# One core, attention with a mixture of experts and a gated MLP behind it: the last head pair in two parts, combine work in late attention, eight output staging buffers, one pass for two w_in quarters, a new order

## The chip, the cores and the metric

The kernel runs on one core of a Trainium2 chip. The metric is the time of one execution on the device in microseconds (us). Five engines work side by side, each through its own list of instructions in order: TensorE (PE; its weight loads are shown apart as PEld), VectorE (DVE), ScalarE (ACT), GpSimd (POOL) and SyncE (SP), which here issues the DMAs. An instruction that waits for another engine holds up everything behind it on its own.

## The reference

Three layers follow each other. Each line is computed in fp32 on 2304 tokens (4 batches of 576) of width 512.

```
scores = q @ k.T / sqrt(64)              # 4 batches x 8 heads, 576 x 576, head size 64
mask:  heads 0-3: 0 <= i-j < 32          # a local window
       heads 4-7: 0 <= i-j < 128 and (i-j) % 4 == 0     # the same, dilated by 4
attn = softmax(masked scores) @ v        # -> x, 2304 x 512
logits = x @ phi                         # 32 slots, 8 experts x 4
slot_in = softmax(logits, over the 2304 tokens).T @ x
slot_out[e] = relu(slot_in[e] @ w1[e]) @ w2[e]          # w1 512 x 1024, w2 1024 x 512
x = softmax(logits, over the 32 slots) @ slot_out
h = x @ w_in;  out = (h * sigmoid(h)) @ w_out           # 512 x 2048, 2048 x 512
```

## The kernel before

**Attention.** A local and a dilated head of a batch make a head pair; there are 16, n = 4b + p. With the dilated head's positions sorted by their rest, both become windows of 64 keys over nine blocks of 64 rows. For each pair: SP loads k, q and v (`lk`, `lq`, `lv`); POOL spreads q into two half-filled tiles (`qx`, `qy`); `vx` (POOL) and `vy` (DVE or ACT) write v twice; PE adds masks and scores (`M`, `S`); DVE takes the row maximum (`rm`); ACT the nine exponentials with their sums (`ex`); DVE the reciprocal (`rc`, L238 and L239), POOL the product with it (`nm`, L242), DVE four transposes (`pt.0` to `pt.3`, L249 to L255); PE multiplies by v (`pv.0`, and `pv.1` for block 0); ACT evicts (`xe`, L280 and L282); PE transposes (`T`, L293) and takes the logits (`lt`); ACT evicts the tokens (`te`).

**Dispatch and combine.** Per batch, `da`, `dt`, `dm`, `db`, `dq`, `dr`, `dsub`, `dex`, `dc`, `dw`, `dacc` and `ds` carry a running softmax over tokens; the last `ds3` gives the slot inputs (`sit`, `sie`). `caa` to `cag` compute the softmax over slots, split into a high and a low part (`cad`, L383; `caf`, L388 and L389). `cb{b}.0` and `cb{b}.1` transpose it on PE for three and for two token tiles (L404), and `cbs` evicts that to `ct`.

**Experts.** `L1.0` to `L1.15` and `L2.0` to `L2.15` run all slots through the experts' halves, with the weights streaming in; `ht` transposes between them, `sotm` behind.

**MLP.** The combine is not done on its own: w_in is multiplied by the slot outputs (`aq`, one eighth of the hidden columns for each q) and stacked as a high and a low part (`ah`, `al`, `ac`, tile `astk`), so that `h` is one matmul of 384 tokens. The weights arrive as 64-bit words and are turned into fp32 by three DVE operations each (`cva`, `cvb`, `cvi` for w_in; `cvc`, `cvd`, `cvo` for w_out: L594, L596, L598); w_out is split too (`wh` on ACT, `wl` on DVE). The work goes in six groups G, of six token tiles and eight hidden tiles f each (groups 0 to 2 with f 0 to 7, groups 3 to 5 with f 8 to 15). A unit is one f for 384 tokens: `h` on PE, `si` on ACT (L758, silu), `gh` on ACT or DVE and `gl` on DVE (L763, L765, L768: the gated value and what its rounding leaves), then three `om` matmuls per token tile (the first unit's are `on`) into six banks. At a group's end `oe` evicts: groups 0 to 2 to `part`, groups 3 to 5 added to it (L850) into an output tile `ost`, from which `do` (SP) stores. There are four places in `ost`.

**What sets the order.** Each piece is an `op` with a name, an engine, a planned cost and the names it depends on. `list_schedule` (L985) plays them through with the costs and the latencies `LAT`, takes on every engine the one with the longest remaining path plus the bonus of its kind in `PRIO`, and keeps PSUM banks apart; `ATT` gives the order of SP's loads. The program then has each engine's instructions in that order. Neither costs nor bonuses are in the program itself.

All matmuls but the transposes and those of `cb` (L404) go through one helper, `mm` (L83), so its line stands for most of PE.

## Time and profile before

| what | us |
|---|---|
| three runs | 367.99, 369.27, 369.54 (median 369.27) |
| the profiled execution | 368.79 |
| its span | 367.0 |
| PE busy in it | 347.6 (95%) |
| DVE busy | 234.6 (64%) |
| ACT busy | 165.9 (45%) |
| POOL busy | 75.3 (21%) |
| granted clock of PE, mean | 0.999 |

The span is the program from its first to its last instruction on the chip; busy times of different engines overlap. In time the program is attention to about 95 us, dispatch to 101, experts to 134.6, the first group of the MLP from 138 to 178 and the other five groups to 363; the last store ends the span at 367.0. A matmul of the 2.4 GHz clock is shown with its modelled end, so the duration of one overlaps with the next; the distance from start to start is the pace.

### The profile page before, as it was taken

The numbers are of one execution on the slowest core, as the hardware profiler recorded it, in microseconds if no ns is written. First come the engines' busy times: TensorE is split into PE (matmuls) and PEld (weight loads), VectorE is DVE, ScalarE is ACT, GpSimd is POOL, SyncE is SP. The second block draws the span as 40 slices with busy tenths as digits, with TensorE's granted clock in tenths as the row PEclk, the third lists the DMA queues.
The fourth block names the chain that finished last, engine by engine and source line by source line (L and its number), as shares of the span: only waits on it lengthen the run. The fifth ranks groups of instructions, "written<-read, shape, count | busy, mean of one in ns | idle before, by whom it ended". The sixth has DMA issues, their size and how long they took to land.

```text
span 367.0 us, 8152 instructions
## 1 busy us (share of the span) xinstructions
PE 347.6 (95%) x3209; PEld 267.6 (73%) x3212; DVE 234.6 (64%) x540; ACT 165.9 (45%) x558; POOL 75.3 (21%) x120
## 2 busy tenths in 40 slices
...
GB/s 258 411 405 404 408 403 402 405 397 287 374 361 424 412 417 417 330 133 0 280 121 59 0 2 0 1 2 0 3 0 0 116 57 0 2 116 56 2 0 171
DMA packets 17461, 70.03 MB, mean 191 GB/s; under 512 B 1936, under 2 KB 2448, under 8 KB 11664
## 3 DMA queue, kind: packets, MB, share of 16 engines
...
q8 instruction: 25, 0.41, 0.5%
q14 instruction: 12, 0.10, 0.1%
HBM read 64.80 MB, written 4.72 MB: 189 GB/s over the span
## 4 chain that ended last, share of the span: by engine, by line
PE 88%; DVE 4%; ACT 3%; issue 2%; POOL 1%; DVEq 0%; ACTq 0%
PE ps L83 85%; PE ps L293 3%; ACT rt_px L226 1%; ACT rt_px L280 1%; PE ps L404 1%; DVE stats L221 1%; DVE w_ost L850 1%; POOL rv_v L189 1%; ACT rt_px L282 1%; POOL rt_px L242 1%; ACT x_xb L296 0%; DVE spaced L222 0%; DVE w_gy L768 0%; DVE rb_a L892 0%; DVE ra_a L892 0%
## 5 line engine op out<-in xcount | busy, mean ns | idle before, releaser
L83 PE MATMUL ps<-w_ws,x_gz 128*128 128x512 f32 x432 | 109.6, 393 | 0.4 <-DVE w_ost L850 0.4
L758 ACT ACTIVATE rt_gtm<-ps 128x384 f32<-128x384 f32 x96 | 46.9, 492 | 105.4 <-PE ps L83 104.3
L83 PEld LDWEIGHTS ps<-w_ws,x_gz 128*128 128x128 f32 x432 | 79.8, 188 | 18.1 <-DVE w_ost L850 1.0
L83 PE MATMUL ps<-w_ws,w_gy 128*128 128x512 f32 (+1 forms) x219 | 56.2, 392 | 1.0 <-DVE w_ost L850 0.4
L226 ACT ACTIVATE rt_px<-ps,spaced 128x64 f32<-128x64 f32 x144 | 43.5, 328 | 12.4 <-DVE spaced L222 7.2
L83 PEld LDWEIGHTS ps<-w_ws,w_gy 128*128 128x128 f32 x219 | 40.1, 188 | 10.7 <-DVE w_ost L850 1.0
L765 DVE CAST x_gz<-rt_gtm 128x384 fp32r<-128x384 f32 x52 | 18.6, 357 | 39.1 <-ACT rt_gtm L758 39.0
L768 DVE TENSOR_TENSOR x_gz<-rt_gtm,x_gz 128x384 fp32r<-128x384 f32 x64 | 35.7, 557 | 4.7 <-ACT rt_gtm L758 0.9
L83 PE MATMUL ps<-ct_ct,rv_astk 128*128 128x384 f32 x96 | 31.6, 335 | 0.0
L226 ACT ACTIVATION_READ_ACCUMULATOR rt_px<-ps,spaced 128x1 f32 x144 | 31.5, 219 | 0.0
L765 DVE CAST w_gy<-rt_gtm 128x384 fp32r<-128x384 f32 x28 | 10.0, 358 | 23.4 <-ACT rt_gtm L758 23.4
L83 PEld LDWEIGHTS ps<-ct_ct,rv_astk 128*128 128x128 f32 x96 | 17.9, 188 | 4.1 <-ACT rv_astk L675 0.2
L242 POOL TENSOR_TENSOR rt_px<-rt_px,stats 128x576 f32<-128x576 f32 x16 | 18.4, 1153 | 9.7 <-DVE stats L239 4.7
L768 DVE TENSOR_TENSOR w_gy<-rt_gtm,w_gy 128x384 fp32r<-128x384 f32 x32 | 17.8, 557 | 2.1
L83 PE MATMUL ps<-rk_ws,x_gz 128*128 128x512 f32 x72 | 18.6, 395 | 0.4 <-ACT x_gz L763 0.4
L83 PE MATMUL ps<-ra_a,rv_v 128*64 128x96 f32 (+2 forms) x320 | 15.3, 241 | 3.7 <-issue 2.0
L221 DVE TENSOR_REDUCE stats<-ps 128x9 f32<-128x576 f32 x16 | 12.0, 753 | 10.1 <-PE ps L83 9.7
L83 PE MATMUL ps<-rb_ws,x_gz 128*128 128x512 f32 x72 | 18.3, 393 | 0.0
L83 PEld LDWEIGHTS ps<-ra_a,rv_v 128*64 128x64 f32 x320 | 13.6, 137 | 5.3 <-issue 2.6
L83 PEld LDWEIGHTS ps<-rk_ws,x_gz 128*128 128x128 f32 x72 | 13.3, 188 | 3.5 <-ACT x_gz L763 0.7
L293 PE MATMUL ps<-ip,rt_px 128*128 128x128 f32 x80 | 12.2, 284 | 3.5 <-ACT rt_px L280 1.8
L83 PEld LDWEIGHTS ps<-rb_ws,x_gz 128*128 128x128 f32 x72 | 13.3, 188 | 2.8 <-issue 0.2
(220 smaller groups left out, 522.7 us busy)
## 6 DMA issues: line engine op xcount, KB each, us to landing
...
```

Of the source, the lines that this page charges most:

```text
L83: pe.matmul(out, lhsT=lhsT, rhs=rhs, start=start, stop=stop, skip_group_check=True)
L189: pool.tensor_copy(out[r, :, z, :], raw[r])
L221: dve.tensor_reduce(out=mxs[:, n % 2], in_=ps[:, c:c + 64 * NJ].rearrange("p (j c) -> p j c", c=64), axis=AXX, op=ALU.max)
L226: act.activation(out=preg(n)[:, j, :], in_=sj(n, j), func=ACTF.Exp, scale=D ** -0.5, bias=nmx[:, r, j // 3, j % 3:j % 3 + 1], accum_out=su ...
L242: pool.tensor_tensor(out=preg(n), in0=preg(n), in1=rinv[:, n % 2].rearrange("p (j o) -> p j o", o=1).to_broadcast([128, NJ, 64]), op=ALU.mult)
L280: act.copy(out=x.rearrange("p (c i) -> p c i", c=4), in_=src.rearrange("p (i c) -> p c i", c=4))
L282: act.copy(out=x, in_=src)
L293: pe.transpose(ps[:, c:c + 128], x[:, tok(t):tok(t) + 128], ident)
L404: pe.transpose(cbank(b, k)[:, c:c + 128 - r0], cc[r0:128, t].rearrange("p r s -> p (r s)"), ident[r0:128, r0:128])
L758: act.activation(out=gtm(u), in_=hb(u), func=ACTF.Silu)
L765: dve.tensor_copy(ghalf(u, 0), gtm(u))
L768: dve.tensor_tensor(out=ghalf(u, 1), in0=gtm(u), in1=ghalf(u, 0), op=ALU.subtract)
```

## The change

- The last pair (n = 15) has its reciprocal, its product and its transposes in two parts, blocks 0 to 5 and 6 to 8 (`rc15.0`, `rc15.1`, `nm15.0`, `nm15.1`, `pt15.0` to `pt15.7`), and its `pv` in three. Its raw v has a tile of its own (`vz`). q has four places throughout; `dm` is laid into another tile (`hsb`).
- `cb` writes to other PSUM banks (`CBANK`), and waits for what was there before instead of for the end of attention (`free`); `caa` too may start earlier.
- `aq2` goes into the pass of `aq3`, as `aq4` and `aq6` already go into those of 5 and 7.
- The output has eight staging places, in two tiles, instead of four.
- The planner has other costs and latencies (`MORE`, `LATE`), a bonus `AHEAD` for `h`, `si`, `gh` and `gl` of the groups after the first, another `PRIO` and another `ATT`; of these tables one or two lines are shown.

```diff
+JH = 6
+CBANK = ((2, 1), (5, 1), (4, 6), (5, 1))
...
+    dm = hsb[0:1, 352:352 + 5 * NS]
+    vz = cp.tile([128, 576], F32, name="vz")
...
+    def qslot(n):
+        return n % 4
...
-        i = rslot(n)
+        i = qslot(n)
         return reg("raw", 576 * i, 576) if i < 2 else reg("more0", 576 * (i - 2), 576)
 
     def vraw(n):
+        if n == NPAIR - 1:
+            return vz
         i = rslot(n)
         return reg("raw", 1152 + 576 * i, 576) if i < 2 else reg("more1", 576 * (i - 2), 576)
...
-    def recip(n):
-        r = n % 2
-        dve.tensor_scalar(out=sume[:, r], in0=sums[:, r].rearrange("p (a b) -> p a b", b=3), scalar1=EPS, scalar2=None, op0=ALU.add)
-        dve.reciprocal(out=rinv[:, r].rearrange("p (a b) -> p a b", b=3), in_=sume[:, r])
-    def normal(n):
-        pool.tensor_tensor(out=preg(n), in0=preg(n),
-                           in1=rinv[:, n % 2].rearrange("p (j o) -> p j o", o=1).to_broadcast([128, NJ, 64]), op=ALU.mult)
-    def ptrans(n, i):
+    def recip(n, j0=0, j1=NJ):
+        r, rows = n % 2, slice(j0 // 3, j1 // 3)
+        dve.tensor_scalar(out=sume[:, r, rows], in0=sums[:, r, j0:j1].rearrange("p (a b) -> p a b", b=3), scalar1=EPS, scalar2=None, op0=ALU.add)
+        dve.reciprocal(out=rinv[:, r, j0:j1].rearrange("p (a b) -> p a b", b=3), in_=sume[:, r, rows])
+    def normal(n, j0=0, j1=NJ):
+        p = preg(n)[:, j0:j1]
+        pool.tensor_tensor(out=p, in0=p,
+                           in1=rinv[:, n % 2, j0:j1].rearrange("p (j o) -> p j o", o=1).to_broadcast([128, j1 - j0, 64]), op=ALU.mult)
+    def ptrans(n, i, j0=0, j1=NJ):
         p = preg(n)
         t = ptreg(n)
         if i == 0:
-            dve.transpose(out=t[0:64, :, 0:32], in_=p[0:64, :, 32:64])
+            dve.transpose(out=t[0:64, j0:j1, 0:32], in_=p[0:64, j0:j1, 32:64])
         elif i == 1:
-            dve.transpose(out=t[0:64, :, 32:64], in_=p[64:128, :, 0:32])
+            dve.transpose(out=t[0:64, j0:j1, 32:64], in_=p[64:128, j0:j1, 0:32])
         elif i == 2:
-            dve.transpose(out=t[64:128, :, 32:64], in_=p[64:128, :, 32:64])
+            dve.transpose(out=t[64:128, j0:j1, 32:64], in_=p[64:128, j0:j1, 32:64])
         else:
-            dve.transpose(out=t[64:128, 0:NJ - 1, 64:96], in_=p[0:64, 1:NJ, 0:32])
+            j0 = max(j0, 1)
+            dve.transpose(out=t[64:128, j0 - 1:j1 - 1, 64:96], in_=p[0:64, j0:j1, 0:32])
...
+        if n == NPAIR - 1:
+            if k == 0:
+                for j in range(1, JH - 1):
+                    one(j, 0, 96, j == 1, False)
+                one(0, 64, 96, False, False)
+            elif k == 2:
+                one(0, 0, 64, True, True)
+            else:
+                for j in range(JH - 1, NJ):
+                    one(j, 0, 96 if j < NJ - 1 else 64, False, j == NJ - 1)
+            return
...
+        if n < NPAIR - 1:
+            op(f"rc{n}", "DVE", .33, [exn(n), f"nm{n-2}" if n >= 2 else None], lambda n=n: recip(n))
+            op(f"nm{n}", "POOL", 1.1, [f"rc{n}"], lambda n=n: normal(n))
+            for i in range(4):
+                op(f"pt{n}.{i}", "DVE", .486, [f"nm{n}", f"pv{n-2}.1" if n >= 2 else f"it{n}"], lambda n=n, i=i: ptrans(n, i))
+            for k in range(2):
+                op(f"pv{n}.{k}", "PE", (1.36, .25)[k], ["fl3" if not n else None] + [f"vx{n}", f"vy{n}"] + [f"pt{n}.{i}" for i in range(4)] + ([(f"xe{n-1}", f"te{n-1}")[k]] if n else []),
+                   lambda n=n, k=k: pv(n, k))
+        else:
+            for k, (j0, j1) in enumerate(((0, JH), (JH, NJ))):
+                op(f"rc{n}.{k}", "DVE", .32, [f"ex{n}.{j1-1}", f"nm{n-2}"], lambda n=n, j0=j0, j1=j1: recip(n, j0, j1))
+                op(f"nm{n}.{k}", "POOL", (.81, .45)[k], [f"rc{n}.{k}"], lambda n=n, j0=j0, j1=j1: normal(n, j0, j1))
+                for i in range(4):
+                    op(f"pt{n}.{i+4*k}", "DVE", (.34, .2)[k], [f"nm{n}.{k}", f"pv{n-2}.1"], lambda n=n, i=i, j0=j0, j1=j1: ptrans(n, i, j0, j1))
+            for k, h in ((0, 0), (2, 0), (1, 1)):
+                op(f"pv{n}.{k}", "PE", (.75, .66, .25)[k], [f"vx{n}", f"vy{n}", f"te{n-1}" if k == 2 else f"xe{n-1}"] + [f"pt{n}.{i+4*h}" for i in range(4)],
+                   lambda n=n, k=k: pv(n, k))
+        op(f"xe{n}", "ACT", .54, [f"pv{n}.1"] + ([f"T{n-2}", f"lt{n-2}"] if n >= 2 else []), lambda n=n: xevac(n))
...
-        return bank[5 if k == 0 else 6 if b == 0 else 1]
+        c = 192 if (b, k) == (1, 1) else 0
+        return bank[CBANK[b][k]][:, c:c + 384 - c]
...
-            prev = [f"cbs{pb}.{k}"] if b else [f"te{NPAIR-1}", f"la{B-1}"]
-            op(f"cb{b}.{k}", "PE", (.45, .3)[k], [f"cag{b}"] + prev + (["db3"] if b == 0 and k else ["he1"] if k else []), lambda b=b, k=k: cb(b, k))
-            op(f"cbs{b}.{k}", "ACT", (.37, .21)[k], [f"cb{b}.{k}", "L1.0" if k == 0 else f"cbs{b}.0"], lambda b=b, k=k: cbe(b, k))
+            e = exn(NPAIR - 1)
+            free = (((e,), (e,)), ((f"xe{NPAIR-1}",), (e,)), ((f"xe{NPAIR-1}", f"te{NPAIR-1}"), (f"la{B-1}", f"da{B-1}")), (("cbs1.0",), ("he1",)))[b][k]
+            op(f"cb{b}.{k}", "PE", (.45, .3)[k], [f"cag{b}", *free], lambda b=b, k=k: cb(b, k))
+            op(f"cbs{b}.{k}", "ACT", (.37, .21)[k], [f"cb{b}.{k}", "cbs0.0" if b or k else "L1.0"], lambda b=b, k=k: cbe(b, k))
...
-        if q < 4 or q % 2:
-            qs = [q] if q < 4 else [q - 1, q]
+        if q % 2:
+            qs = [q] if q == 1 else [q - 1, q]
             before = [f"al{x}" for x in range(max(q - 3, 0), qs[0])] + (["alr0"] if q == 1 else [])
             op(f"aq{q}", "PE", 1., [f"cvi{x}.{k}" for x in qs for k in range(2)] + before, lambda qs=qs: aq(qs))
...
-        op(f"ah{q}", "ACT", .16, [f"aq{q if q < 4 else q | 1}"] + lastc, lambda q=q: ahc(q))
+        op(f"ah{q}", "ACT", .16, [f"aq{q | 1}"] + lastc, lambda q=q: ahc(q))
...
-        if "ost" not in tiles:
-            new("w10", "ost")
-        return reg("ost", (i % 4) * 512, 512)
+        k, place = (("ost", "w10"), ("osu", "ra"))[i % 8 // 4]
+        if k not in tiles:
+            new(place, k)
+        return reg(k, (i % 4) * 512, 512)
...
-                op(f"oe{x}", "DVE", .6 / n, [f"om{G}.{t}.{f0 + FH - 1}", f"do{i-4}" if i >= 4 else "cvi6.1", f"oe{G}.{t}" if k else None],
+                op(f"oe{x}", "DVE", .6 / n, [f"om{G}.{t}.{f0 + FH - 1}", f"do{i-8}" if i >= 8 else "aq3" if i > 3 else "cvi6.1", f"oe{G}.{t}" if k else None],
...
+AHEAD = 3.0
...
-VY = ("DVE", "ACT")
+VY = ("DVE", "ACT", "DVE", "ACT")
...
-PRIO = {'T': 2.22, 'nm': 6.74, 'om': -1, 'cae': -2, ...
+PRIO = {'T': 3.55, 'nm': 5.02, 'om': -0.5, 'cae': 0, ...
...
-    bonus = lambda n: PRIO.get(n.rstrip("0123456789."), 0.0)
+    ahead = lambda k, n: AHEAD if k in ("h", "si", "gh", "gl") and n[len(k)] != "0" else 0.0
+    bonus = lambda n: PRIO.get(n.rstrip("0123456789."), 0.0) + ahead(n.rstrip("0123456789."), n)```

The order of DVE near the start of the program, before; `ra_a0_108` is pair 0's transposed P, `L221` is the row maximum and `L238`, `L239` are the reciprocal:

```order
L193 TENSOR_SCALAR rv_v_111<-rs_raw_112,zm_74 128x9x64
L221 TENSOR_REDUCE stats_77<-ps_81 128x9
L222 TENSOR_SCALAR spaced_78<-stats_77 128x3x3
L249 STREAM_TRANSPOSE ra_a0_108<-rt_px_113 64x9x32
L238 TENSOR_SCALAR spaced_78<-stats_77 128x3x3
L239 RECIPROCAL stats_77<-spaced_78 128x9
L251 STREAM_TRANSPOSE ra_a0_108<-rt_px_113 64x9x32
L253 STREAM_TRANSPOSE ra_a0_108<-rt_px_113 64x9x32
L255 STREAM_TRANSPOSE ra_a0_108<-rt_px_113 64x8x32
```

And the same place in the new order, where the row maximum is `L229` and the reciprocal `L246`, `L247`:

```order
L201 TENSOR_SCALAR rv_v_111<-rs_raw_112,zm_74 128x9x64
L258 STREAM_TRANSPOSE ra_a0_108<-rt_px_113 64x9x32
L260 STREAM_TRANSPOSE ra_a0_108<-rt_px_113 64x9x32
L262 STREAM_TRANSPOSE ra_a0_108<-rt_px_113 64x9x32
L265 STREAM_TRANSPOSE ra_a0_108<-rt_px_113 64x8x32
L246 TENSOR_SCALAR spaced_78<-stats_77 128x3x3
L247 RECIPROCAL stats_77<-spaced_78 128x9
L229 TENSOR_REDUCE stats_77<-ps_81 128x9
L230 TENSOR_SCALAR spaced_78<-stats_77 128x3x3
```

Pair 0's four transposes have moved ahead of pair 1's reciprocal and pair 2's row maximum.

DVE in the first group of the MLP, before; `w15_wi2` and `w16_wi3` are the raw words of w_in's parts q = 2 and q = 3, `ra_wif1` is where both go, and `L594`, `L596`, `L598` are the three steps of a conversion:

```order
L598 SCALAR_TENSOR_TENSOR ra_wif1_2044<-w15_wi2_1938,ra_wif1_2044 128x512
L596 SCALAR_TENSOR_TENSOR ra_wif1_2044<-w15_wi2_1938,ra_wif1_2044 128x512
L768 TENSOR_TENSOR x_gz_1985<-rt_gtm_1992,x_gz_1985 128x384
L598 SCALAR_TENSOR_TENSOR ra_wif1_2044<-w15_wi2_1938,ra_wif1_2044 128x512
L594 TENSOR_SCALAR w9_wt_1890<-rs_wo2_1981 128x512
L594 TENSOR_SCALAR ra_wif1_2044<-w16_wi3_2006 128x512
L596 SCALAR_TENSOR_TENSOR w9_wt_1890<-rs_wo2_1981,w9_wt_1890 128x512
L768 TENSOR_TENSOR x_gz_1985<-rt_gtm_1992,x_gz_1985 128x384
L653 TENSOR_TENSOR lg_65<-ps_81,chi_69 64x128
L598 SCALAR_TENSOR_TENSOR w9_wt_1890<-rs_wo2_1981,w9_wt_1890 128x512
L594 TENSOR_SCALAR w9_wt_1890<-rs_wo2_1981 128x512
L594 TENSOR_SCALAR ra_wif1_2044<-w16_wi3_2006 128x512
```

The same place in the new order, with `L633`, `L635` and `L637` as the steps of a conversion:

```order
L633 TENSOR_SCALAR ra_wif1_2027<-w16_wi3_2002 128x512 x2
L807 TENSOR_TENSOR w8_gy_2000<-rt_gtm_1996,w8_gy_2000 128x384
L637 SCALAR_TENSOR_TENSOR ra_wif1_2027<-w15_wi2_1940,ra_wif1_2027 128x512
L807 TENSOR_TENSOR w8_gy_2000<-rt_gtm_1996,w8_gy_2000 128x384
L635 SCALAR_TENSOR_TENSOR ra_wif1_2027<-w15_wi2_1940,ra_wif1_2027 128x512
L635 SCALAR_TENSOR_TENSOR ra_wif1_2027<-w16_wi3_2002,ra_wif1_2027 128x512
L637 SCALAR_TENSOR_TENSOR ra_wif1_2027<-w15_wi2_1940,ra_wif1_2027 128x512
L637 SCALAR_TENSOR_TENSOR ra_wif1_2027<-w16_wi3_2002,ra_wif1_2027 128x512
L635 SCALAR_TENSOR_TENSOR ra_wif1_2027<-w16_wi3_2002,ra_wif1_2027 128x512
L637 SCALAR_TENSOR_TENSOR w9_wt_1873<-w14_wo1_1931,w9_wt_1873 128x512
L637 SCALAR_TENSOR_TENSOR ra_wif1_2027<-w16_wi3_2002,ra_wif1_2027 128x512
L807 TENSOR_TENSOR x_gz_1999<-rt_gtm_1996,x_gz_1999 128x384
```

All six steps of q = 3 now stand among and right behind the last of q = 2, ahead of w_out's part 2 (`rs_wo2`); before, four of them came later than the rows shown.

DVE at the end of the program, before; `L765` and `L768` are the gating steps (`gh`, `gl`), `L850` the evictions of the last group:

```order
L765 CAST w8_gy_1986<-rt_gtm_1992 128x384
L768 TENSOR_TENSOR w8_gy_1986<-rt_gtm_1992,w8_gy_1986 128x384
L850 TENSOR_TENSOR w10_ost_3099<-ps_81,w16_part3_2839 128x512 x2
L765 CAST w8_gy_1986<-rt_gtm_1992 128x384
L850 TENSOR_TENSOR w10_ost_3099<-ps_81,w16_part3_2839 128x512
L768 TENSOR_TENSOR w8_gy_1986<-rt_gtm_1992,w8_gy_1986 128x384
L850 TENSOR_TENSOR w10_ost_3099<-ps_81,w16_part3_2839 128x512
L850 TENSOR_TENSOR w10_ost_3099<-ps_81,rs_part4_2864 128x512
L850 TENSOR_TENSOR w10_ost_3099<-ps_81,rs_part4_2864 128x256 x2
```

The end in the new order (`L804` and `L807` are the gating steps, `L890` is the eviction):

```order
L804 CAST w8_gy_2000<-rt_gtm_1996 128x384
L807 TENSOR_TENSOR w8_gy_2000<-rt_gtm_1996,w8_gy_2000 128x384
L804 CAST w8_gy_2000<-rt_gtm_1996 128x384
L807 TENSOR_TENSOR w8_gy_2000<-rt_gtm_1996,w8_gy_2000 128x384
L890 TENSOR_TENSOR ra_osu_3135<-ps_81,w16_part3_2834 128x512 x4
L890 TENSOR_TENSOR w10_ost_3110<-ps_81,rs_part4_2864 128x512
L890 TENSOR_TENSOR w10_ost_3110<-ps_81,rs_part4_2864 128x256 x2
```

The gating steps of the last unit have moved ahead of the first eviction of the group.

## Rows read from the trace of the kernel before

**Rows 1.** The page: the chain that ended last, shares of the span by engine.

```profile
PE 88%; DVE 4%; ACT 3%; issue 2%; POOL 1%; DVEq 0%; ACTq 0%
```

**Rows 2.** Windows, four stages: length, busy PE, PEld, DVE, ACT, POOL, clock, DMA share, GB/s.

```profile
26.87:90.43 63.56, 57.24 (x1275) 49.65 (x1275) 45.42 (x121) 52.94 (x250) 44.06 (x63) 1.00 1.00 394
90.43:101.29 10.86, 9.09 (x161) 6.97 (x156) 6.89 (x28) 4.23 (x9) 3.79 (x8) 1.00 0.82 331
...
138.47:178.40 39.93, 39.92 (x209) 31.85 (x209) 38.61 (x76) 26.91 (x69) 0.00 (x0) 1.00 0.57 220
178.40:363.13 184.73, 183.25 (x866) 149.44 (x864) 110.40 (x232) 56.92 (x129) 0.00 (x0) 1.00 0.10 39
```

**Rows 3.** Waits of PE, 26.87 to 90.43: total us, times, longest us.

```profile
PE ps L83 <- issue: 2.9, 3, 2.0
PE ps L293 <- ACT rt_px L280: 1.5, 3, 0.8
PE ps L293 <- ACT rt_px L282: 1.4, 3, 0.7
```

**Rows 4.** The page's DMA queues: packets, MB, share of 16 engines' time.

```profile
q8 instruction: 25, 0.41, 0.5%
```

**Rows 5.** Windows of two blocks and of one, in attention; columns as in rows 2.

```profile
39.40:52.90 13.50, 11.12 (x255) 9.45 (x255) 9.56 (x27) 9.66 (x46) 10.24 (x14) 1.00 1.04 410
71.48:77.17 5.69, 5.55 (x135) 5.12 (x132) 4.90 (x14) 5.17 (x29) 3.81 (x5) 1.00 0.98 388
```

**Rows 6.** Timeline, 5 to 24: start us, us, instruction, [idle before <- releaser].

```profile
12.73 1.16 POOL L242 TENSOR_TENSOR rt_px<-rt_px,stats 128x576 f32<-128x576 f32 x1 [0.49 <-DVE stats L239]
...
15.28 0.46 DVE L249 STREAM_TRANSPOSE ra_a<-rt_px 64x288 f32<-64x288 f32 x1
...
17.54 1.58 PE L83 MATMUL ps<-ra_a,rv_v 128*64 128x96 f32 x36 [1.40 <-DVE ra_a L255]
```

**Rows 7.** Timeline of PE at the end of attention.

```profile
95.12 0.49 PE L83 MATMUL ps<-rt_px,ip 128*32 128x128 f32 x12 [0.38 <-ACT rt_px L282]
...
97.32 0.55 PE L404 MATMUL ps<-ip,cc 128*128 128x128 f32 x3
```

**Rows 8.** Timeline of DVE there.

```profile
95.34 0.49 DVE L389 TENSOR_TENSOR cc<-cn,chi 128x320 f32<-128x320 f32 x1
```

**Rows 9.** Timeline of PE in the experts, 105.5 to 124.4: the combine's transposes.

```profile
106.58 0.55 PE L404 MATMUL ps<-ip,cc 128*128 128x128 f32 x3
...
123.84 0.51 PE L404 MATMUL ps<-ip,cc 128*128 128x128 f32 x2
```

**Rows 10.** Timeline of PE in the MLP: the pass of q = 2, a joint pass.

```profile
153.34 1.26 PE L83 MATMUL ps<-ra_wif,lg 128*32 128x128 f32 x16
...
242.46 1.08 PE L83 MATMUL ps<-w_wif,lg 128*32 128x128 f32 x32
```

**Rows 11.** Groups by form, DVE, 138.47 to 178.40: busy us, mean ns, idle before.

```profile
L596 DVE SCALAR_TENSOR_TENSOR ra_wif<-w_wi,ra_wif 128x512 uint32<-128x512 uint32 x4 | 2.7, 685 | 0.0
...
L594 DVE TENSOR_SCALAR ra_wif<-w_wi 128x512 uint32<-128x512 uint32 x4 | 1.7, 420 | 0.0
```

**Rows 12.** Timeline of ACT at the first unit of the MLP.

```profile
138.69 0.50 ACT L758 ACTIVATE rt_gtm<-ps 128x384 f32<-128x384 f32 x1
```

**Rows 13.** Timeline of PE at the end of group 3 (at group 4's end: 329.44).

```profile
292.84 0.96 PE L83 MATMUL ps<-w_ws,w_gy 128*128 128x512 f32 x3 [0.43 <-DVE w_ost L850]
```

**Rows 14.** Timeline of PE: in group 1, and the end of the program.

```profile
209.97 1.85 PE L83 MATMUL ps<-w_ws,x_gz 128*128 128x512 f32 x6
...
356.14 1.52 PE L83 MATMUL ps<-w_ws,x_gz 128*128 128x512 f32 x6
...
359.03 0.86 PE L83 MATMUL ps<-w_ws,w_gy 128*128 128x512 f32 x3
360.17 0.73 PE L83 MATMUL ps<-w_ws,w_gy 128*128 128x512 f32 x2 [0.28 <-DVE w_gy L765]
361.23 1.90 PE L83 MATMUL ps<-w_ws,w_gy 128*128 128x512 f32 x10 [0.33 <-DVE w_gy L768]
```

92 lines of the change are left out of this document (48 added, 44 removed).

## The prediction

> **What bounds the kernel now.** I read the page's chain of waits first: 88% of the span is TensorE (PE), and VectorE (DVE), ScalarE (ACT) and "issue" share most of the rest [rows 1]. So only what PE loses counts, and the windows by stage show where [rows 2]: attention's main part, 26.87 to 90.43, holds 57.24 us of PE work in 63.56 us; its end, up to the first expert matmul at 101.29, holds 9.09 in 10.86; the opening of the MLP, 138.47 to 178.40, has PE full (39.92 of 39.93) but DVE nearly so too (38.61); the rest, 184.73 us, has PE at 183.25. The 6.3 us lost in the main part come next, from the waits of PE there: issue 2.9 in three waits, the longest 2.0, and six waits of a T step for its xe, 1.5 and 1.4 together [rows 3]. In an issue wait PE waits for nothing that the profile names. The page has 25 instruction fetches, 0.41 MB [rows 4], that is 16 KB each, and counted in the order of PE the three waits stand where its instructions pass a multiple of 256 behind a fixed offset. I therefore read the stage as blocks of 256 PE instructions (a matmul is two of them, the weight load and the multiply): ten blocks fill 26.87 to 90.43, 6.36 us each. The two between 39.40 and 52.90 hold the longest wait and took 13.50 for 11.12 us of PE work, 6.75 each; the quickest, 71.48 to 77.17, took 5.69 and has no such wait; in both the DMA engines were busy without a gap [rows 5].
>
> The sum is made against the profiled execution: 368.79 us, of which 367.0 is span. That is 0.48 under the median of the runs shown, 369.27, and inside their 367.99 to 369.54; I let the two stand for each other.
>
> **The change part by part.** Start: pair 0's P is normalised by 12.73 + 1.16 = 13.89, but its four transposes run from 15.28, behind pair 2's row maximum and with pair 1's reciprocal among them; pv0.0 waits 1.40 us for the last of them, from 16.14 [rows 6]. In the new order they stand right behind the vector work that precedes. Four of 0.46 from 13.9 end near 15.8, so the wait goes: **-1.4**. Late next are pair 2's row maximum, some 1.7 us later, and the nine exponentials behind it; if these then hold PE, nothing is won. Bounds 0 and -1.5; I take the row.
>
> Main part: the new order puts masks and scores of later pairs between a pv and the T that needs its xe, so most of the 2.9 us for xe would go. But PE then comes to its block edges sooner, and a block is not there before it has been fetched. For the pace that the fetches allow I take the middle of the slow and the quick blocks, 6.2: ten take 62.0, -1.6; I halve that, since the edges now fall on other steps: **-0.8**. Bounds: PE's own 57.24 (-6.3), and ten blocks as slow as the two above, 67.5 (+3.9).
>
> The Trainium skill ("Runtime: NRT & Kernel Launch", section "Instruction fetch mechanics") says that instructions are refilled in blocks of 256 and that crossing a boundary is mostly hidden. The block size agrees with the 16 KB a fetch here [rows 4]; the hiding does not, with one wait of 2.0 us. By that rule the pace of 6.2 would fall away, which is rival A.
>
> End of attention: before the first expert matmul PE now does the combine transposes (cb) of two batches instead of one, two groups more, 0.55 [rows 7] for three matmuls and some 0.4 for two: +0.95. They fill the wait of 0.38 for the last xe [rows 7]: -0.38. T14 has nothing ahead of it any more that covers xe14, since a small matmul and lt13 went further ahead: +0.75, near the longest such wait, 0.8 [rows 3]. And ds3, on which the slot inputs and so the experts wait, has two more combine steps ahead of it on DVE, the larger of 0.49 [rows 8]; DVE has idle time there, so I take half, +0.25 (0 to 0.8). The last pair in two parts wins nothing: PE has just reached its pv when the whole pair's transposes are done. It adds four transposes, at most 0.46 each [rows 6], a reciprocal and a normalisation on engines that have room, DVE with 6.89 and POOL with 3.79 of 10.86 us busy [rows 2]: 0, and without that cover 0.8, the four transposes less what each is shorter for half the columns. The last pair's own v tile, the fourth q slot and the combine's other banks issue nothing on PE, and of the loads, which stand in another order on SP, PE waits for none in [rows 3]; POOL, whose spreads a late q would hold, has 19.5 us free in the main part [rows 2]: 0. Together **+1.6** (0 to +3).
>
> Experts: the two groups that move ahead took 0.55 and 0.51 [rows 9] in a stage where PE has no room; one matmul of each overlaps with its neighbour, so **-0.95**.
>
> MLP opening: the pass for w_in 2 joins that for 3. A pass alone is 16 matmuls of 1.26 us in all, a joint pass as there is one at 242.46 takes 1.08 for 32 [rows 10], so one pass goes: -1.25. The price is on DVE: the six conversion steps of q = 3 now stand ahead of the pass that q = 2 had to itself. One of them came right behind it anyway; the others, one of 0.42 and four of 0.685 [rows 11], are 3.2 us pulled ahead on an engine that has 1.3 us free in 39.93 [rows 2]. Walking along the new order with these durations, PE waits about 1.1 for the joint pass, 0.6 for the copies into astk behind it and 0.65 for two gated columns: +2.35. The first output matmul has one more silu ahead of its gating step on ACT, 0.5 [rows 12] less some overlap: +0.4. Later, in group 1, a wait for a gated column goes, 0.33, as six matmuls take 1.85 us there and 1.52 elsewhere [rows 14]: -0.3. Together **+1.2** (-1 to +4).
>
> Boundaries: at the ends of groups 3 and 4 the next group's output matmul waits 0.43 for an eviction from its bank [rows 13], and loses the 0.2 by which such matmuls else overlap (0.42 long at 0.22 apart, from [rows 14] as below). On DVE those evictions stand among the gating steps now, and with eight staging buffers none has to wait for a store. Both waits go, nearly twice 0.63: **-1.2**. Bounds 0 and -1.26.
>
> Tail: matmuls follow each other by 0.22 ((1.52 - 0.86) / 3), but the group of three at 359.03 has its successor 1.14 later and that group of two its own 1.06 later [rows 14]: 0.48 + 0.62 lost, since the last gating steps stand behind and among evictions on DVE. The new order has both gating steps ahead of the first eviction: **-1.1**. The eviction and the store after the last matmul stay. Bounds 0 and -1.1.
>
> Sum: -1.4 - 0.8 + 1.6 - 0.95 + 1.2 - 1.2 - 1.1 = -2.65; 368.79 - 2.65 = 366.1, **366.1 us**.
>
> **The rivals.** A, the block fetch does not bind. For it: seven of ten blocks pass without an issue wait, one of them in 5.69. Against it: the waits stand exactly at block edges. Then the main part could shrink towards its 57.24; ACT, busy for 52.94 of the 63.56 us [rows 2], lets it come to some 59.8 by my walk, -3.8 instead of -0.8: 363.1, and with T14's wait covered as well, 362.4. I say 362.4. Chance 0.15.
>
> B, DVE in the MLP's opening costs more. Each conversion that is late holds PE for 0.685, with 1.3 us of slack for 3.2 us moved ahead; waits twice as long as counted, 4.7 for 2.35, give 366.1 + 2.35 = 368.5, no change. For it: DVE's 38.61 of 39.93. Against: the conversions are the same in number. Chance 0.15.
>
> C, the slower side: fetches. The DMA engines have no gap in attention [rows 5] and the fetch of a block has to pass there too; if PE, which now comes early to its edges, meets each fetch as late as between 39.40 and 52.90, ten blocks take 67.5 instead of 62.8, and the block that follows loses another 0.5: 366.1 + 5.2 = 371.3. It is slower than before from 6.6 us a block on, (369.27 - 366.1) / 10 over 6.28. For it: that pair of blocks. Against: the 5.69, with DMA as full. Chance 0.10, of which a bit more than half lies beyond 371.1.
>
> **How the numbers follow.** The forecast, with its own range of 363.3 to 367.4, has 0.60; A 0.15, B 0.15, C 0.10. A measurement of this kernel can tell about 0.5%, 1.85 us, from no change: faster is below 367.4, slower above 371.1. Faster is the forecast and A, 0.75; within 0.5% B and the nearer part of C, 0.19; slower the rest of C, 0.06. The range goes down to 361.9, where part of A is left out, and up to 369.2, which takes in B with the dear end of its waits and leaves out C.
>
> **What the new profile would show.** Right: no wait of 1.4 us at the first pv; fewer waits of T for xe, but issue waits at other steps, the scores of pairs 8 and 9, pv10 and pv3, where the block edges now fall; four combine groups before the first expert matmul; a wait of about 1 us ahead of the joint pass; no wait of PE for an eviction at the two boundaries and none for a gating step in its last 4 us. Wrong: a main part under 60.5 us without issue waits (A), PE waiting over 4 us in the MLP's opening (B), issue waits of over 6 us (C), or S and T waiting for the exponentials that the early transposes have pushed back.

## The result and the profile after

The changed kernel takes 364.77 us, median of six runs (363.40 to 366.18), against 369.08 before, also of six; the ratio is 0.9884, with a 95% interval of 0.9846 to 0.9923. The profiled execution took 365.69, its span 363.8 (before: 368.79 and 367.0). The forecast was 366.1, range 361.9 to 369.2: it was right, if 1.3 too high, but some of its terms were not, and two large errors among them cancel.

Where the time went, by the starts and ends of the same steps in three traces. The third is a variant with the changed kernel's order (four output places instead of eight, which the experiments show to cost 0.1 at most), in which the clock stayed up:

| step, at us | before | changed | four places |
|---|---|---|---|
| T1 starts | 25.06 | 22.79 | 22.65 |
| T14 starts | 91.91 | 89.32 | 88.62 |
| first expert matmul | 101.29 | 100.75 | 99.44 |
| last expert matmul ends | 134.07 | 134.25 | 132.57 |
| first output matmul | 138.47 | 139.01 | 137.34 |
| group 1's first | 178.40 | 178.77 | 177.06 |
| group 5's first | 325.57 | 324.52 | 322.81 |
| last output matmul ends | 363.13 | 359.96 | 358.25 |

The last expert matmuls in the three traces; in the third, four of the eight wait for the load of the last weight:

```profile
133.03 1.04 PE L83 MATMUL ps<-w_w2.15_1847,x_sip 128*32 128x512 f32 x8
133.01 1.24 PE L86 MATMUL ps<-w_w2.15_1888,x_sip 128*32 128x512 f32 x8
131.52 1.05 PE L86 MATMUL ps<-w_w2.15_1888,x_sip 128*32 128x512 f32 x4 [0.16 <-DMA w_w2.15_1888<-in_w]
```

Windows of the changed kernel by stage; the first covers the same number of blocks as that of [rows 2], ten, by the same count. Columns: length, busy PE, PEld, DVE, ACT, POOL, clock, DMA share, GB/s.

```profile
24.05:87.10 63.05, 58.03 (x1275) 50.07 (x1277) 46.89 (x131) 52.67 (x255) 44.97 (x66) 1.00 1.02 404
87.10:100.75 13.65, 11.22 (x167) 8.26 (x163) 10.26 (x39) 4.72 (x11) 5.93 (x12) 0.85 1.00 403
139.01:178.77 39.76, 39.53 (x210) 31.31 (x211) 38.87 (x77) 26.35 (x68) 0.00 (x0) 1.00 0.62 244
178.77:359.96 181.19, 181.19 (x865) 149.97 (x863) 108.39 (x228) 56.32 (x128) 0.00 (x0) 1.00 0.09 34
```

Ten blocks still take 63.05 us. The last 181 us have no idle PE at all, where [rows 2] has 1.5 lost. The second line has a clock of 0.85, where the windows of [rows 2] have 1.00. PE's waits in the ten blocks (total, times, longest) answer to [rows 3]:

```profile
PE ps L86 <- issue: 3.3, 5, 1.2
PE ps L86 <- DVE rb_a L265: 1.0, 1, 1.0
PE ps L314 <- ACT rt_px L301: 0.4, 1, 0.4
```

The waits of T for xe, 2.9 before, are 0.4; the issue waits stayed, and there are five now instead of three. In the chain of waits four of them stand at the scores of pairs 8 and 9 (42.40 and 49.15), at pv10 and at the scores of pair 14, where the block edges now fall; the fifth, 0.26, is at pv8 (56.18):

```profile
42.40 1.22 issue
49.15 0.99 issue
...
68.40 0.51 issue
74.35 0.38 issue
```

The start, for [rows 6]: the transposes begin at 12.96, pv0.0 at 15.25 without a wait.

```profile
12.96 0.47 DVE L258 STREAM_TRANSPOSE ra_a<-rt_px 64x288 f32<-64x288 f32 x1 [0.74 <-POOL rt_px L251]
...
15.25 1.72 PE L86 MATMUL ps<-ra_a,rv_v 128*64 128x96 f32 x40
```

The end of attention on PE, for [rows 7]. L437 is cb: five matmuls, two, three, so two batches. T14 waits 0.78 for xe14, and the last row, dc3, is slow:

```profile
89.32 0.76 PE L314 MATMUL ps<-ip,rt_px 128*128 128x128 f32 x5 [0.78 <-ACT rt_px L303]
...
92.09 0.86 PE L437 MATMUL ps<-ip,cc 128*128 128x128 f32 x5
...
95.56 0.53 PE L437 MATMUL ps<-ip,cc 128*128 128x128 f32 x2
...
96.33 0.55 PE L437 MATMUL ps<-ip,cc 128*128 128x128 f32 x3
96.82 2.53 PE L86 MATMUL ps<-x_xb,le 128*32 128x129 f32 x40
```

Windows of 2 us there, with the columns as above:

```profile
92.00:94.00 2.00, 2.00 (x28) 1.47 (x24) 1.19 (x6) 0.64 (x1) 0.73 (x2) 1.00 0.94 381
94.00:96.00 2.00, 1.28 (x8) 0.65 (x6) 1.28 (x5) 0.72 (x2) 1.20 (x3) 1.00 0.98 381
96.00:98.00 2.00, 2.00 (x30) 1.70 (x33) 1.13 (x7) 0.83 (x3) 0.40 (x1) 0.69 1.03 426
98.00:100.00 2.00, 1.52 (x25) 0.67 (x17) 1.30 (x4) 0.00 (x0) 0.61 (x2) 0.50 1.00 414
100.00:102.00 2.00, 1.55 (x9) 0.40 (x13) 0.84 (x5) 0.00 (x0) 2.00 (x3) 0.50 0.87 356
```

After 2 us in which PE was busy for 1.28, the granted clock fell to 0.5, the 1.2 GHz level, from 96.7 to 103.6. dc3 took 2.53 us (1.45 before), the first two expert matmul groups 1.71 and 1.41 from start to start (0.88 and 0.86 before). The joint pass, a boundary and the end of the program, for [rows 10, 13, 14]:

```profile
153.73 1.41 PE L86 MATMUL ps<-ra_wif,lg 128*32 128x128 f32 x32
```

```profile
290.22 2.23 PE L86 MATMUL ps<-w_ws,w_gy 128*128 128x512 f32 x9
```

```profile
355.69 4.27 PE L86 MATMUL ps<-w_ws,w_gy 128*128 128x512 f32 x21
```

The profile shows no wait of PE in these. The joint pass is longer than the 1.08 of [rows 10], and has a break of 0.2 in its middle: its second half starts at 154.50, right behind the last step of the conversion of q = 3 on DVE:

```profile
153.76 0.69 DVE L637 SCALAR_TENSOR_TENSOR ra_wif<-w_wi,ra_wif 128x512 uint32<-128x512 uint32 x1
```

From the first output matmul on PE waits twice, 0.7 us in all, the 0.5 of it ahead of that first matmul:

```profile
PE ps L86 <- ACT x_gz L802: 0.5, 1, 0.5
PE ps L86 <- ACT rv_astk L714: 0.2, 1, 0.2
```

### The profile page after: what moved, and what is told of

Its sections match the earlier page's. It is cut to its first block, busy times and chain, and to the rows that moved or that the text cites. A ratio compares the mean times of both kernels' runs of the same rounds, so it can differ in the third digit from the quotient of the medians.

```text
span 363.8 us, 8145 instructions
## 1 busy us (share of the span) xinstructions
PE 348.5 (96%) x3212; PEld 268.1 (74%) x3212; DVE 234.8 (65%) x546; ACT 164.3 (45%) x558; POOL 74.2 (20%) x121
## 3 DMA queue, kind: packets, MB, share of 16 engines
HBM read 64.80 MB, written 4.72 MB: 191 GB/s over the span
## 4 chain that ended last, share of the span: by engine, by line
PE 73%; DMA 10%; DVE 8%; ACT 5%; issue 2%; SPq 1%; POOL 0%; DVEq 0%; ACTq 0%; POOLq 0%
PE ps L86 70%; DMA w_wo<-in_w_out 4%; DMA rs_raw<-in_v 3%; DMA w_more<-in_k 2%; PE ps L314 2%; DMA rk_k<-in_k 1%; ACT rv_astk L714 1%; ACT rt_gtm L797 1%; ACT w_ws L669 1%; DVE ra_wif L637 1%; ACT rt_px L234 1%; ACT x_gz L802 1%; PE ps L437 1%; DVE w_wif L637 1%; DVE w_wif L635 1%
## 5 line engine op out<-in xcount | busy, mean ns | idle before, releaser
L86 PE MATMUL ps<-w_ws,x_gz 128*128 128x512 f32 x432 | 109.0, 392 | 0.1
L86 PEld LDWEIGHTS ps<-w_ws,x_gz 128*128 128x128 f32 x432 | 80.2, 188 | 16.8 <-DVE x_gz L807 0.5
L86 PE MATMUL ps<-w_ws,w_gy 128*128 128x512 f32 (+1 forms) x219 | 55.2, 389 | 0.0
L86 PEld LDWEIGHTS ps<-w_ws,w_gy 128*128 128x128 f32 x219 | 40.4, 188 | 8.2 <-issue 0.2
L804 DVE CAST x_gz<-rt_gtm 128x384 fp32r<-128x384 f32 x52 | 18.6, 358 | 40.1 <-ACT rt_gtm L797 40.0
L807 DVE TENSOR_TENSOR x_gz<-rt_gtm,x_gz 128x384 fp32r<-128x384 f32 x64 | 35.6, 557 | 5.1 <-PE ps L86 0.5
L234 ACT ACTIVATION_READ_ACCUMULATOR rt_px<-ps,spaced 128x1 f32 x144 | 33.3, 232 | 0.0
L86 PE MATMUL ps<-ct_ct,rv_astk 128*128 128x384 f32 x96 | 31.7, 339 | 0.2 <-ACT rv_astk L714 0.2
L804 DVE CAST w_gy<-rt_gtm 128x384 fp32r<-128x384 f32 x28 | 10.0, 357 | 18.8 <-ACT rt_gtm L797 18.8
L86 PEld LDWEIGHTS ps<-ct_ct,rv_astk 128*128 128x128 f32 x96 | 18.0, 188 | 5.1 <-ACT rv_astk L714 0.5
L251 POOL TENSOR_TENSOR rt_px<-rt_px,stats 128x576 f32<-128x576 f32 (+2 forms) x17 | 18.6, 1094 | 11.0 <-DVE gmx L453 3.6
L807 DVE TENSOR_TENSOR w_gy<-rt_gtm,w_gy 128x384 fp32r<-128x384 f32 x32 | 17.8, 558 | 2.6 <-ACT w_gy L802 0.4
L86 PE MATMUL ps<-rk_ws,x_gz 128*128 128x512 f32 x72 | 18.5, 395 | 0.5 <-ACT x_gz L802 0.5
L86 PE MATMUL ps<-rb_ws,x_gz 128*128 128x512 f32 x72 | 18.3, 394 | 0.0
L229 DVE TENSOR_REDUCE stats<-ps 128x9 f32<-128x576 f32 x16 | 11.9, 744 | 6.8 <-PE ps L86 4.7
L86 PE MATMUL ps<-ra_a,rv_v 128*64 128x96 f32 (+2 forms) x320 | 15.1, 241 | 0.8 <-issue 0.8
L86 PEld LDWEIGHTS ps<-rk_ws,x_gz 128*128 128x128 f32 x72 | 13.3, 188 | 3.5 <-ACT x_gz L802 0.8
L86 PEld LDWEIGHTS ps<-ra_a,rv_v 128*64 128x64 f32 x320 | 13.6, 137 | 2.6 <-issue 1.2
L86 PEld LDWEIGHTS ps<-rb_ws,x_gz 128*128 128x128 f32 x72 | 13.3, 188 | 2.8 <-DVE rb_ws L758 0.2
L86 PE MATMUL ps<-rb_a,rv_v 128*64 128x96 f32 (+2 forms) x320 | 14.4, 241 | 1.0 <-DVE rb_a L265 1.0
```

The source lines that it names most:

```text
L86: pe.matmul(out, lhsT=lhsT, rhs=rhs, start=start, stop=stop, skip_group_check=True)
L229: dve.tensor_reduce(out=mxs[:, n % 2], in_=ps[:, c:c + 64 * NJ].rearrange("p (j c) -> p j c", c=64), axis=AXX, op=ALU.max)
L234: act.activation(out=preg(n)[:, j, :], in_=sj(n, j), func=ACTF.Exp, scale=D ** -0.5, bias=nmx[:, r, j // 3, j % 3:j % 3 + 1], accum_out=su ...
L251: pool.tensor_tensor(out=p, in0=p, in1=rinv[:, n % 2, j0:j1].rearrange("p (j o) -> p j o", o=1).to_broadcast([128, j1 - j0, 64]), op=ALU.mult)
L804: dve.tensor_copy(ghalf(u, 0), gtm(u))
L807: dve.tensor_tensor(out=ghalf(u, 1), in0=gtm(u), in1=ghalf(u, 0), op=ALU.subtract)
```

## The experiments

All start from the changed kernel and keep its order of instructions, word for word, but for the edit. Single runs are read by stage, since an execution varies by a us or two.

**Attention: what paces the ten blocks?** First, half the PE instructions for the products with v.

```diff
-            for z in range(2):
-                mm(ps[64 * z:64 * z + 64, c + c0:c + c1], v[:, j, z], t[:, j, c0:c1], start, stop)
+            mm(ps[:, c + c0:c + c1], v[:, j].rearrange("p z c -> p (z c)"), t[:, j, c0:c1], start, stop)
```

> The changed kernel with the two 64-column halves of v used as one 128-column weight: each product with v takes half the PE instructions for the same result, 40 instead of 80 per head pair, so attention's ten blocks of 256 become about eight. Theory F (the fetch of PE's blocks paces attention: 63.0 us for ten blocks between 24.05 and 87.1 in the changed kernel): the waits called issue go, and T1 to T14, 66.5 us apart there (22.79 to 89.32), come 3 to 5 us nearer, 61.5 to 63.5; the time falls to about 361. Rival X (the chain of exponentials, transposes and products paces it, and the block edges only coincide): 66.5 within 0.5, time 364.8. Rival P (a product with 128 columns costs PE more than two with 64): 68 or more, slower than the changed kernel.

369.49 us, 1.0019 of the kernel before (0.9993 to 1.0045). T1 to T14 took 70.7: rival P's number. A product with 128 columns of v costs more: 20 matmuls in 2.34 us where 40 took 1.72. But of 3.3 us of issue waits none is left between 24 and 94; these are all of PE's waits there:

```profile
PE ps L313 <- ACT rt_px L300: 0.4, 1, 0.4
PE ps L86 <- DVE rb_a L265: 0.2, 1, 0.2
```

So the waits go when instructions take longer each (256 of them take some 8.5 us here, an estimate from 2117 in 69.93 us); the time can't show F here. Second, the weights out of the way of attention:

```diff
 order:
-lv4 lw1.2 ... lw1.14 ... lv15 lw1.15
+lv4 ... lv15 lw1.1 lw1.2 ... lw1.15
```

> The changed kernel's order, but the expert weights w1.1 to w1.15 are loaded behind the last v, so that attention has the DMA engines nearly for itself; the experts then wait for their weights and the whole is far slower (over 380 us), only attention is to be read. Theory F with a fetch that is slow because the DMA engines are full: the waits called issue go and T1 to T14 fall from 66.5 us to 61.5 to 64. Theory F2 (the fetch has its own pace of some 6 us a block whatever else the DMA engines do): 66 to 66.5 with issue waits of 3 us as now. Rival X (another chain paces attention): 66.5, and few issue waits.

T1 to T14 fell from 66.5 to 62.9, the ten blocks from 63.05 to 59.5. Of the issue waits one is left, 0.9 from 76.7 on, when the weights load again. The two windows show the DMA share (second column from the end) without and with them:

```profile
31.00:42.00 11.00, 10.56 (x252) 9.05 (x249) 9.31 (x25) 10.09 (x54) 8.43 (x15) 1.00 0.44 151
70.00:84.00 14.00, 12.72 (x271) 10.57 (x267) 11.85 (x37) 11.98 (x56) 9.53 (x14) 1.00 1.00 407
```

That is F as written, and F2 and X fail: blocks come late because the DMA engines are full. The loads of q, k and v come earlier here too; from T1 to T14 no wait of PE for them is seen in either kernel.

The traces also hold the fetches themselves, one packet of 16 KB each on queue q8 of [rows 4]. In the changed kernel's attention a fetch takes 1.0 to 1.1 us, and starts 3.2 to 4.5 us after PE has passed a block edge; from 35 to 85 us they follow each other by 6.0 to 6.4. Each of the five issue waits ends 1.3 to 1.6 us after a fetch has landed (the first: fetch from 41.21 to 42.33, PE goes on at 43.62). With the weights out of the way, from 31 to 66 us, a fetch starts within 1.2 us of its edge and has landed 3.2 us or more before the next. The fetch ahead of the one wait left starts 5.0 us after its edge, at 75.11, and the wait ends 1.5 us after it has landed. In pv_half_instr, with the DMA engines full as well, every fetch of attention lands 4.4 us or more before the edge. So the issue waits are waits for the fetch of a block.

**The start.** Pair 0's transposes behind the row maximum, and the filler's operand set late:

```diff
-pt0.0 pt0.1 pt0.2 pt0.3 rc1 rm2 pv0.0
+rm2 pt0.0 rc1 pt0.1 pt0.2 pt0.3 pv0.0
```

> The changed kernel with pair 0's four transposes moved back behind pair 2's row maximum and, but for the first, behind pair 1's reciprocal, as before. If this order gave the start its gain: pv0.0 starts about 1.1 us later (16.3 instead of 15.25) and T1, T14 shift by about as much, 0.8 to 1.1. Rival: a later wait takes it up (pv3.0 waits 1.0 us for its own transposes): T14 moves by less than 0.3.

```diff
-lq0 ifl iza0 izb0 pex fl0 iza1 lk0 iq0 izb1
+lq0 iza0 izb0 iza1 lk0 iq0 izb1 ifl pex fl0
```

> The changed kernel with the fill of the first dummy matmuls' operand moved back behind the two q memsets on DVE, as before. If its place gave part of the gain of the start: the first dummy matmuls begin at 2.4 instead of 1.2 us, the first scores take about 2.2 us again instead of 1.27 and end near 7.6 instead of 6.26, pv0.0 comes 1.0 later, and T14 as well. Rival: the wait for q and the exponentials take it up, T14 within 0.3.

The first brings the wait back, 1.40, and T1 comes 1.62 later, but T14 only 0.22 (89.54), below the rival's 0.3. In the second the scores end at 6.96, not 7.6, and T1 moves 0.1, T14 0.15: the expectation missed, and the place of the fill is worth no more than this, within what two executions differ by. In the first:

```profile
17.28 1.72 PE L86 MATMUL ps<-ra_a,rv_v 128*64 128x96 f32 x40 [1.40 <-DVE ra_a L265]
...
30.22 1.58 PE L86 MATMUL ps<-rb_a,rv_v 128*64 128x96 f32 x36 [0.40 <-DVE rb_a L265]
```

A part is taken up at pv3.0, which waits 0.40 instead of 1.03, the rest at the block edges: S8 and S9 wait 0.9 and 0.7 there in the chain, for 1.2 and 1.0, and the wait of 0.38 at S14 is gone.

**The boundaries: the buffers or the order?**

```diff
-f"do{i-8}" if i >= 8 else "aq3" if i > 3 else "cvi6.1"
+f"do{i-4}" if i >= 4 else "cvi6.1"
```

> The changed kernel in its own order, with four staging places for the output instead of eight, each eviction waiting for the store four before it. Theory O (the new order of DVE at the ends of groups 3 and 4 took PE's waits away, the buffers did not): in the changed kernel the fifth eviction starts at 288.4, and the first store, issued at 286.0, takes some 2 us, so nothing waits there; only at the end of the program the fifth and sixth eviction wait some 0.3 us; span 0 to 0.5 longer. Theory B (the eight buffers did it): PE waits of 0.4 us for an eviction come back at both ends, span 0.8 to 1.3 longer.

364.29, span 362.3. From group 4's first output matmul to group 5's 35.84 us pass and from there to the last 35.44, both as with eight; the end behind it is 0.1 longer. Theory O holds.

**The tail.**

```diff
-gh5.15.1 gl5.15.1 ... oe5.0 oe5.1 oe5.2
+... oe5.0 oe5.1 gh5.15.1 oe5.2 gl5.15.1
```

> The changed kernel with the last gating steps (gh5.15.1, gl5.15.1) moved back behind the second and third eviction of the last group, as before. If their place made the gain at the tail: PE waits for gl5.15.1 ahead of its last nine matmuls or so, 0.9 to 1.2 us, and the span from the first output matmul of the last group (324.5 in the changed kernel) to the end grows from 39.3 to 40.2 to 40.5. Rival: the evictions, not the gating, end last, and the end stays within 0.2 of 39.3.

```profile
356.62 0.73 PE L86 MATMUL ps<-w_ws,w_gy 128*128 128x512 f32 x2 [0.37 <-DVE w_gy L804]
357.68 1.89 PE L86 MATMUL ps<-w_ws,w_gy 128*128 128x512 f32 x10 [0.33 <-DVE w_gy L807]
```

The picture of [rows 14] is back, and the stretch to the last output matmul takes 36.70 for 35.44: +1.26, a little above what was expected.

**The combine's place.**

```diff
-cb1.1 dr3 cb1.0 ... caf2 ... L1.0 L1.1 L1.2 L1.3 L1.4
+dr3 ... L1.0 L1.1 L1.2 L1.3 L1.4 cb1.1 cb1.0 caf2
```

> The changed kernel with the combine transposes of batch 1 (and what hangs on them: the combine steps of batches 2 and 3 that follow) moved back behind the fifth expert matmul group. Theory P (PE bounds this stretch, as the prediction's sum has it): the first expert matmul comes 0.9 to 1.3 earlier, relative to the products with v of the last pair, and the last expert matmul ends the same 0.0 to 0.4 earlier, since the two groups cost the experts 0.95 again. Theory D (the loads of the expert weights bound it: the last weight lands near 132.5 in every run, and the last expert matmul waits for it): the last expert matmul ends within 0.5 of 133.1 to 134.0 whatever comes before; a first expert matmul that is earlier lets its buffer go and that load start earlier, by at most what the DMA engines stand idle at 102 to 106.

From T14 to the first expert matmul 9.88 us pass, 0.7 to 1.1 less than the 10.6 to 11.0 of the runs of the full clock. The experts then took 34.53, for 31.92 at full clock where no weight is late; the clock was down at their start, 1.5 by the first two groups, which leaves 1.1, near the 0.95 of the two combine groups. That is theory P. D's "whatever comes before" fails: with the changed order of loads the last expert matmul ended between 131.5 and 134.7 (137.4 in pv_half_instr). But D has a part: it ended 30.0 to 30.3 us behind the second group in seven of the eleven runs with the changed order here, and 30.6 to 31.2 behind it in the other four; in the one shown above (four places) PE waits for the last weight.

**One load moved behind the weights** (with its conversion behind w_in's):

```diff
-lw2.13 lwo1 lw2.14 lw2.15 lwi0.1 lw2b lwi0.2 lwi1.0
+lw2.13 lw2.14 lw2.15 lwi0.1 lw2b lwi0.2 lwo1 lwi1.0
```

> The changed kernel with the load of the second half of w_out's first part (512 KB, some 1.25 us at 410 GB/s) moved behind the last expert weights and w_in's first part, and its conversion on DVE behind that of w_in. Theory D (loads bound the experts): the last expert matmul ends 0.7 to 1.2 us earlier than in a run with the same clock (133.1 without the slow clock: 132.0 to 132.4; with it 134.0: 132.9 to 133.2), and the first output matmul 0.5 to 1.2 earlier; the 2.5 us of conversions then fall into the MLP's opening, where DVE has little room, and may take it back. Theory P (PE bounds it): the last expert matmul stays.

366.72. The last expert matmul ended at 132.00, as D had it, but still 30.0 behind the second group, which P has as well: it does not tell them apart. The first output matmul came at 140.11, 3.3 later behind it than in the changed kernel. Half of that is a wait of 1.63 ahead of the first pass for w_in, whose copies on ACT now stand behind the converted tile of w_out; the other half is the clock, which fell to 0.5 from 135.4 to 138.8, so that this pass took 3.53 for 1.95:

```profile
134.42 0.62 ACT L669 CAST rk_ws<-w_wt 128x512 fp32r<-128x512 f32 x1 [1.71 <-DVE w_wt L637]
134.95 0.32 ACT L594 COPY lg<-ps 128x64 f32<-128x64 f32 x2
135.21 3.53 PE L86 MATMUL ps<-w_wif,lg 128*32 128x128 f32 x64 [1.63 <-ACT lg L594]
```

**The pass for w_in 2.**

```diff
-lambda qs=qs: aq(qs))
+lambda qs=qs: [aq([x]) for x in qs] if qs == [2, 3] else aq(qs))
```

> The changed kernel with w_in 2 and 3 in two passes of 16 matmuls one behind the other at the place of the joint pass. The prediction's step: a pass costs PE 1.25, so the first group of the MLP, first output matmul to the next group's first (39.7 in the changed kernel), takes 0.9 to 1.3 more. Rival: PE waits for the conversions of q = 3 there anyway, and the pass hides in that wait: less than 0.3 more.

```profile
152.05 1.54 PE L86 MATMUL ps<-ra_wif,lg 128*32 128x128 f32 x32
```

1.54 for 1.41, and the group takes 39.86 for 39.76. The number is the rival's, but not its cause: PE does not wait there for long (the break of 0.2 above). Two passes back to back overlap for the most part: 1.54 for both, where one alone takes 1.26 or 1.07.

**The last pair in one part.**

```diff
-        if n == NPAIR - 1:
+        if False:
...
-        if n < NPAIR - 1:
+        if True:
```

> The changed kernel with the last pair's reciprocal, product, transposes and products with v in one part, all else in the changed kernel's order. The prediction's step (PE is the bound there, the split wins nothing): from T14 to T15 4.05 as now, within 0.2. Rival W: the last transpose then ends near 91.0 instead of 90.0 for the first four and 91.2 for the rest, PE's last product waits for it by about 0.5, and T14 to T15 takes 4.4 to 4.7.

```profile
90.80 1.73 PE L86 MATMUL ps<-rb_a,rv_v 128*64 128x96 f32 x40 [0.38 <-DVE rb_a L265]
```

T14 to T15 takes 4.49: rival W. But T14 to the first expert matmul takes 10.74, with the split 10.60 to 10.97 at full clock: what the split wins is waited for again behind T15.

**The clock.** Dummy matmuls in the waits between T15 and the experts:

```diff
+    for i in range(6):
+        op(f"fz{i}", "PE", .225, ["te15"] if i < 2 else ["dw3"], lambda: mm(bank[0], identb, maskb[:, 0:512], True, True))
-T15 ... dt3 ... db3 ... sit ... L1.0
+T15 ... fz0 dt3 ... fz1 db3 ... fz2 fz3 sit ... fz4 fz5 L1.0
```

> The changed kernel with six dummy matmuls of 512 columns (0.21 us each) in PE's waits between the last T of attention and the first expert matmul: one before dt3, one before db3, two before sit, two before the first expert matmul. In its profiled execution the changed kernel ran at a granted clock of 0.5 to 0.6 from 96.9 to 104, and two of its six executions show a mean clock of 0.989. Theory C (PE's thin work from 94 to 96.8 lets the clock fall, and the fall costs about 1.6 us where it happens): no stretch at 0.5 in this profile, clock 0.998 or more, from T15 to the first expert matmul 6.8 us instead of 7.4, median 363.6 to 364.4. Rival: the clock falls all the same, or the dummy matmuls cost in each run what they save in some: median 364.8 or more.

```profile
94.00:96.00 2.00, 1.95 (x11) 1.19 (x10) 0.84 (x4) 0.98 (x3) 0.70 (x2) 1.00 1.03 434
96.00:98.00 2.00, 2.00 (x45) 1.16 (x43) 1.39 (x9) 0.29 (x1) 0.68 (x2) 1.00 1.00 418
```

364.14 median, 0.9857 of before (0.9832 to 0.9882); all five executions had a mean clock of 0.998 or more, of the changed kernel four in six. The kernel before has a lower mean clock in some executions too: of the nine runs beside these, the two at 1.000 took 367.7, the seven at 0.994 or 0.995 took 369.0 to 370.2; where it fell in them no trace shows. Theory C fits, but the gain over the changed kernel, 0.6, lies within the intervals. Nor is it shown that the thin work brings the fall: work as thin did not bring it in the kernel before (first line) nor in filler_late and gate_behind_evict, at the place itself:

```profile
100.00:102.00 2.00, 1.05 (x11) 0.43 (x13) 1.32 (x6) 0.00 (x0) 1.83 (x2) 1.00 1.04 438
94.00:96.00 2.00, 1.21 (x9) 0.63 (x7) 1.26 (x4) 0.69 (x1) 1.15 (x3) 1.00 0.94 352
94.00:96.00 2.00, 1.20 (x9) 0.63 (x7) 1.26 (x4) 0.69 (x1) 1.19 (x3) 1.00 0.94 373
```

**All that pointed to a gain, together** (the six dummy matmuls are in it as well).

```diff
-lt13 pv14.0 ... pv14.1 ... T14      si0.0.0 gh0.0.0 si0.0.1 gh0.0.1
+pv14.0 ... pv14.1 ... lt13 T14      gh0.0.0 si0.0.0 gh0.0.1 si0.0.1
```

> The changed kernel with the six dummy matmuls, with lt13 moved back to right before T14 (which waits 0.78 for xe14 there), and with the first unit's gating step ahead of its silu on ACT again (the first output matmul waits 0.5). If PE is the bound at both places: T14 0.3 earlier or lt13 hidden, the first output matmul 0.35 nearer to the last expert matmul (5.0 to 4.65), no slow clock: median 363.2 to 364.0. If the loads or the block fetch take up what PE gains there: 364.3 to 364.8.

```profile
88.98 0.76 PE L314 MATMUL ps<-ip,rt_px 128*128 128x128 f32 x5 [0.38 <-ACT rt_px L303]
```

363.73 median (363.25 to 364.49), 0.9851 of before (0.9825 to 0.9878): the fastest here, and not told apart from the changed kernel. T14's wait fell from 0.78 to 0.38, and the first output matmul came 0.4 earlier behind the experts, but its group then took 40.12 for 39.76: given back.

## Why the prediction was right, point by point

- **Start, -1.4, and main part, -0.8.** T14 came 2.6 earlier, 2.2 were forecast. But the two are not a sum. At T1 the start gave 2.3; a start 1.6 worse cost T14 0.2, so what the start wins is mostly taken up, in part where the prediction looked, at block edges. The main part's order alone gives 1.7: T1 to T14 is 65.1 in the run with the old start, 66.85 before. The pace taken for a block, 6.2 us, was 6.3, and 6.2 with the old start. Of the issue waits named, the one at pv3 did not come: pv3.0 waits 1.03 for its own transposes.
- **Rival A** fell: the blocks bind. The rule of the Trainium skill ("Runtime: NRT & Kernel Launch", "Instruction fetch mechanics") that a block's boundary is mostly hidden holds in the runs where the DMA engines have room (at a share of 0.44 there was no wait) and where PE takes longer over a block (pv_half_instr, some 8.5 us); it does not hold in the changed kernel, where a share of 1.02 went with 3.5 us in five waits of up to 1.2 and one of 0.2.
- **Rival C** fell: ten blocks took 63.05, not 67.5.
- **End of attention, +1.6.** T14 to the first expert matmul took 9.38 before, 10.6 to 11.0 at full clock: +1.2 to +1.6. The clock added 0.5 to 0.8 in the profiled run, which no term had.
- **The split at 0**: right in the net; its reason, that PE is the bound, was wrong (the whole pair's transposes hold PE by 0.38).
- **Experts, -0.95.** Where no weight was late and the clock was up, -0.86 (31.92 for 32.78): the reason was right. But a late last weight made it up to 33.1 in other runs of the full clock, and in the profiled run, with the clock down for two groups, it was +0.7. No term had either.
- **MLP opening, +1.2.** This is the mis-sized step: -0.4 was measured (+0.4, -0.2 and, for group 1, -0.6). The first output matmul came 0.4 later behind the experts, as forecast, but the group took 0.17 less, where 1.1 more were forecast. The waits, 2.35, came to 0.2, and the wait of 1 us ahead of the joint pass, named as a sign, did not come. DVE had done the low parts of w_out's first two tiles at 128.6 and 131.8 instead of 132.4 and 138.4, so two steps of the next conversion of w_in (1.37 in all) ran from 137.5 on, ahead of the first output matmul, instead of from 140.6 on, behind it; and DVE left the low part of the fourth tile until 155.5 instead of 151.6. So there was room for q = 3. I had counted DVE's room from 138 on, as if what stood before stayed. That this is the cause is read from the traces; no run puts the old order back. The pass, -1.25, was mis-sized too: 1.41 for the joint one against 1.26 + 1.07 for the two apart is -0.9. With the waits that makes -0.7 for the group; the 0.5 to the measured -0.17 is in part one `h` matmul that now falls into this group, and for the rest stays open. Rival B fell with the waits.
- **Group 1, -0.3**: -0.56.
- **Boundaries, -1.2, and tail, -1.1.** From group 4's first output matmul to group 5's, which holds one boundary, 0.76 were won, and 2.12 from there to the last, which holds the other and the tail; the tail is 1.26 by its own experiment. So 1.6 and 1.26, both beyond the bounds that the prediction gave, 1.26 and 1.1. The order did it; the buffers, which the prediction named with it, are worth 0.1 at the end of the program.

Sum over the profiled executions: -2.59 (to T14) + 2.05 (to the experts) + 0.72 (experts) + 0.36 - 0.17 (MLP opening) - 0.56 - 0.10 (groups 1 to 3) - 0.76 - 2.12 = -3.17, from 363.13 to 359.96 at the last output matmul; the end behind it is the same within 0.03. That the forecast of -2.65 comes within 0.5 of this is in part luck: the experts came out 1.7 dearer than forecast, mostly by the clock, and the MLP opening 1.6 cheaper. In the trace at full clock (the table's third column) the gain is 4.7, 2.1 more than forecast: 0.7 of what it has over the profiled run stand at T14 already, 2.0 come from there to the end of the second expert group, and 1.0 of that is given back where the last expert matmul waits for its weight.
